# Second operands of an MoE input product: split straight out of PSUM or passed through DRAM as ready hi and lo pairs

## The chip, the cores and the metric

The kernel runs on one core of one Trainium2 chip. Its engines work side by side, each through its own queue in order: TensorE (PE, matrix products into PSUM), VectorE (DVE), ScalarE (ACT), GpSimd (POOL), and SyncE (SP), which issues the DMAs here. The metric is the device time of one execution in microseconds.

## The reference

An attention without learned projections over 8 batches of 8 heads (S = 512 tokens x, Ns = 32 state rows, D = 64) is read both ways, its heads are put side by side, and the rows go through a two-layer network with a squared ReLU:

```python
scores = scale * np.matmul(x, state.transpose(0, 1, 3, 2))
a = softmax(scores);  xread = np.matmul(a, state)         # 512 rows a batch
scores2 = scale * np.matmul(state, x.transpose(0, 1, 3, 2))
a2 = softmax(scores2);  sread = np.matmul(a2, x)          # 32 rows a batch
x = concat(xread, sread) as (8 * 544) rows of 512
h = np.maximum(x @ w_in, 0.0)                             # w_in 512 x 2048
return (h * h @ w_out).astype(np.float32)                 # w_out 2048 x 512
```

x and state come as float32, w_in and w_out as float64.

## The kernel before, in words

Every product is made of three TensorE matmuls (`mm3`): each fp32 operand is split into a hi part, which one fp32r holds, and a lo part, the rest; hi by hi, hi by lo and lo by hi are summed in PSUM. A split (`split`, lines 302 to 304) is a cast on ScalarE for hi and a subtraction on POOL or VectorE for lo.

The read of x by the states is folded into w_in: for a batch, `a @ (state @ w_in)` takes the place of `(a @ state) @ w_in`. The product of a batch's states with w_in is called **W2**, a matrix of 256 rows (8 heads of 32 state rows) by 2048 columns. There are nine blocks of tokens: block b, 0 to 7, is the x read of batch b (512 tokens, two operand tiles of 128 rows from W2), and block 8 the 256 rows of the state reads of all batches (four tiles of 128 rows of w_in itself). A block runs through 16 column chunks `fc` of 128: `hidden` makes the squared ReLU of a chunk with six matmuls of 512 columns (block 8: twelve of 256), splits it into g_hi (ScalarE, line 743) and g_lo (VectorE, line 744), and `accumulate` adds its product with w_out's rows into four PSUM banks (twelve matmuls of 512). Blocks 0 and 1 run chunks 0 to 7 first and park their sums in DRAM (`part_d`), then chunks 8 to 15.

w_in comes in 16 pieces p of 256 rows by 256 columns (two to a column block hb of 256). `load_raw` loads one, `decode_wi` turns its float64 words into fp32 with one ScalarE and four VectorE operations (lines 332 to 336) and stores it to DRAM (`win_d`). The 16 pieces of w_out are decoded the same way (`prep_wo`, tile names deco and wo).

W2 is made in one of two ways. **Direct** (`split_wi`, `direct_w2`): the piece is split, and the states of two batches stand in block-diagonal form, six matmuls of 256 columns for a p; ScalarE copies the result from PSUM (tile w2o), SyncE stores it in `w2a_d`. For batch 0 the copy is split on the spot; for others `load_w2` loads it back (tile w_f) and splits it. **Quad** (`quad_load`, `quad_prep`, `quad_w2`): the hi of 64 rows stands over the lo of the same 64 rows in one tile (tt), and four batches' states are multiplied at once, eight matmuls of 256 for a p; the results (qo) go to DRAM, are loaded and split. Batches 0 and 1 with 6 and 7 use the first way for p 0 to 7; for p 8 to 15 the quad (6, 7, 0, 1). Batches 2 to 5 are a quad throughout. `load_wi` loads pieces of w_in for block 8 in another row order and splits them.

The order of the work is written by hand: `PLAN` is a text that lists the steps in the order in which they are traced, and `step` checks their needs; the tile framework then sets the order on each engine by a cost model of its own. `SECOND` names the steps whose second choice of engine is taken (a split's subtraction on VectorE in place of POOL).

## Time and profile before

| | |
|---|---|
| median of 3 runs | 746.01 us (744.4 to 748.93) |
| profiled execution | 745.6 us, span 743.8 us |
| mean granted clock of TensorE | 0.970 |
| busy PE, DVE, ACT, POOL | 689.0, 450.0, 425.8, 252.6 us |
| moved by DMA | 94.10 MB |

A line of a profile names an engine, an operation, the tile that it writes and those that it reads, the shape, and how many; `ph` is a hidden chunk in PSUM, `acc` an accumulator, `w2ps` and `qps` the PSUM tiles of the two ways of W2, `k` the attention weights, `dec` a decoded piece of w_in, `xn` the tokens for the state read. L304 is line 304, a split's subtraction, which all splits share; so the tile names tell them apart. "idle before" is time in which that engine stood, with the work that ended it.

### The profile page before, as it was taken

Reading aid. Unit: us, or ns where it says so; the run is one execution under the profiler, and the core shown is the slowest. Engines: PE = TensorE matmul, PEld = TensorE weight load, DVE = VectorE, ACT = ScalarE, POOL = GpSimd, SP = SyncE. Lnnn points to the kernel's source line nnn. Section 1 sums busy time; section 2 is a strip of 40 time slices with the busy share of each in tenths; the row PEclk is TensorE's granted clock in tenths of the full one; section 3 lists DMA queues with packets and bytes.
Section 4 is the critical chain, followed back from the end, with each engine's and each line's share of the span. In section 5 each row is a group of like instructions: output and inputs, shape, how many; then the busy total and the mean of one; then the engine's idle time right before and its main releaser. Section 6 shows DMA issues by size and latency. Waiting matters only on the chain.

```text
span 743.8 us, 9790 instructions
## 1 busy us (share of the span) xinstructions
PE 689.0 (93%) x3240; PEld 568.6 (76%) x3240; DVE 450.0 (60%) x735; ACT 425.8 (57%) x824; POOL 252.6 (34%) x214
## 2 busy tenths in 40 slices
...
GB/s 267 210 197 183 189 188 254 212 139 231 147 210 222 114 240 115 149 123 148 66 100 83 145 92 65 57 113 80 35 57 143 29 42 57 128 58 71 15 1 85
DMA packets 85331, 94.10 MB, mean 127 GB/s; under 512 B 27681, under 2 KB 59425, under 8 KB 85281
## 3 DMA queue, kind: packets, MB, share of 16 engines
...
q8 instruction: 25, 0.41, 0.2%
...
## 4 chain that ended last, share of the span: by engine, by line
PE 63%; DVE 17%; DMA 7%; issue 5%; ACT 4%; SPq 2%; POOL 1%; DVEq 0%; ACTq 0%; POOLq 0%
PE acc L322 37%; PE ph L322 19%; PE pr L322 2%; DVE dec L335 2%; DVE deco L335 2%; DMA w_f<-w_d 2%; DVE g_lo L744 1%; DMA w_d<-qo 1%; PE st L322 1%; DVE deco L336 1%; DVE dec L333 1%; DVE dec L336 1%; PE w2ps L322 1%; DVE tt L676 1%; DMA wo_raw<-in_moe_w_out_dram 1%
## 5 line engine op out<-in xcount | busy, mean ns | idle before, releaser
L322 PE MATMUL acc<-wo,g_hi 128*128 128x512 f32 x1088 | 321.4, 398 | 16.7 <-ACT g_hi L743 15.5
L322 PEld LDWEIGHTS acc<-wo,g_hi 128*128 128x128 f32 x1088 | 205.4, 192 | 60.7 <-ACT g_hi L743 17.3
L322 PE MATMUL acc<-wo,g_lo 128*128 128x512 f32 x544 | 189.6, 392 | 0.0
L744 DVE TENSOR_TENSOR g_lo<-ph,g_hi 128x512 fp32r<-128x512 f32 (+1 forms) x144 | 94.3, 655 | 102.1 <-ACT g_hi L743 101.5
L322 PEld LDWEIGHTS acc<-wo,g_lo 128*128 128x128 f32 x544 | 102.0, 190 | 20.8 <-issue 0.5
L742 DVE SCALAR_TENSOR_TENSOR ph<-ph,r 128x512 f32<-128x512 f32 (+1 forms) x98 | 65.2, 666 | 79.9 <-ACT r L741 79.4
L743 ACT CAST g_hi<-ph 128x512 fp32r<-128x512 f32 (+1 forms) x144 | 80.8, 563 | 56.7 <-DVE ph L742 54.9
L322 PE MATMUL ph<-k_hi,w_hi 128*128 128x512 f32 x256 | 102.5, 402 | 10.6 <-DVE g_lo L744 8.3
L322 PE MATMUL ph<-k_lo,w_hi 128*128 128x512 f32 x256 | 101.2, 395 | 0.4 <-DVE k_lo L304 0.4
L322 PE MATMUL ph<-k_hi,w_lo 128*128 128x512 f32 x256 | 100.5, 393 | 0.3 <-POOL w_lo L304 0.3
L304 POOL TENSOR_TENSOR w_lo<-w_f,w_hi 128x512 fp32r<-128x512 f32 x39 | 51.9, 1331 | 137.9 <-ACT w_hi L303 134.3
L741 ACT ACTIVATE r<-ph 128x512 f32<-128x512 f32 (+1 forms) x98 | 56.3, 575 | 50.3 <-PE ph L322 49.9
L303 ACT CAST w_hi<-w_f 128x512 fp32r<-128x512 f32 x60 | 37.2, 621 | 67.2 <-PE ph L322 45.5
L322 PEld LDWEIGHTS ph<-k_hi,w_hi 128*128 128x128 f32 x256 | 48.5, 190 | 23.4 <-DVE g_lo L744 8.7
L322 PEld LDWEIGHTS ph<-k_hi,w_lo 128*128 128x128 f32 x256 | 48.6, 190 | 11.1 <-POOL w_lo L304 0.7
L322 PEld LDWEIGHTS ph<-k_lo,w_hi 128*128 128x128 f32 x256 | 48.8, 190 | 9.7 <-DVE k_lo L304 0.8
L676 POOL TENSOR_TENSOR tt<-decq,tt 64x512 fp32r<-64x512 f32 x16 | 21.3, 1331 | 46.7 <-ACT tt L673 27.9
L737 ACT ACTIVATE ph<-ph 128x512 f32<-128x512 f32 (+1 forms) x46 | 25.4, 553 | 16.2 <-PE ph L322 16.0
L304 POOL TENSOR_TENSOR xn_lo<-xn,xn_hi 128x1024 fp32r<-128x1024 f32 x10 | 24.4, 2439 | 26.0 <-ACT xn_hi L303 19.9
L304 POOL TENSOR_TENSOR x_lo<-xT,x_hi 128x512 fp32r<-128x512 f32 x11 | 14.8, 1342 | 51.6 <-DVE sp L424 32.5
L304 POOL TENSOR_TENSOR s<-decs,s 128x512 fp32r<-128x512 f32 x12 | 16.3, 1367 | 38.5 <-ACT s L303 38.4
L686 PE MATMUL qps<-tt,s_hi 128*128 128x256 f32 x96 | 25.6, 291 | 1.6 <-DVE qo L312 1.4
...
## 6 DMA issues: line engine op xcount, KB each, us to landing
w_d<-qo SPq DMA_DIRECT2D x96, 128.0 KB, 2.2
w_f<-w_d SPq DMA_DIRECT2D x48, 256.0 KB, 2.8
wo_raw<-in_moe_w_out_dram SPq DMA_DIRECT2D x16, 512.0 KB, 5.0
wi_raw<-in_moe_w_in_dram SPq DMA_DIRECT2D x16, 512.0 KB, 4.2
out_dram<-o SPq DMA_DIRECT2D x32, 256.0 KB, 3.9
xp<-in_x_dram SPq DMA_DIRECT2D x48, 128.0 KB, 2.6
decq<-win_d SPq DMA_DIRECT2D x24, 256.0 KB, 2.6
xn<-in_x_dram SPq DMA_DIRECT2D x12, 512.0 KB, 3.6
```

What stands on the lines that cost most here:

```text
L303: nc.scalar.copy(hi, src)
L304: pick(key, nc.gpsimd, nc.vector).tensor_sub(lo, src, hi.bitcast(F32))
L322: m = nc.tensor.matmul(ps, l, r, start=first and i == 0, stop=last and i == len(seq) - 1)
L335: nc.vector.scalar_tensor_tensor(v, high, 0xC0000000, v, ALU.bitwise_and, ALU.bitwise_or)
L336: nc.vector.scalar_tensor_tensor(v, low, 29, v, ALU.logical_shift_right, ALU.bitwise_or)
L676: eng.tensor_sub(t[v, :, i], wf[u], t[u, :, i].bitcast(F32))
L686: nc.tensor.matmul(ps[:, h2], s4_hi[:, h], t[:, c, h2], start=True, stop=False)
L737: nc.scalar.activation(ph, ph, AF.Relu)
L741: nc.scalar.activation(r, ph, AF.Relu)
L742: nc.vector.scalar_tensor_tensor(ph, ph, 0.0, r, ALU.max, ALU.mult)
L743: nc.scalar.copy(ghi, ph)
L744: nc.vector.tensor_sub(glo, ph, ghi.bitcast(F32))
```

## The change

w_in passes through DRAM as hi and lo: `split_wi` splits all 16 pieces once (POOL makes the lo of all but the first), and its tile, twice the bytes, is what is stored to `win_d`. What is loaded from there needs no conversion: `quad_load` puts the quad's operand together with four loads of 64 partitions, `load_wi` fills hi and lo with eight loads a tile pair, and `quad_prep` is gone.

For batches 0 and 1, p 0 to 7, `direct_w2` multiplies with the whole block-diagonal states, twelve matmuls of 256 columns for a p, and splits the result out of PSUM: hi by a ScalarE copy, lo by a VectorE subtraction, 128x256 for each batch. Batch 1's tiles lie in the buffers of w_out's last four pieces, whose loads therefore stand behind block 1's hidden chunks 1, 3, 5 and 7. For p 8 to 15 of batches 0 and 1, and for all p of batches 6 and 7, `paired_w2` takes six matmuls, splits out of PSUM (128x512) and stores hi and lo; `load_w2` then loads pairs without a split. Batches 2 to 5 remain a quad, with their split after the load. By count TensorE has 80 matmuls more (of 256 columns), VectorE 733 instructions for 737, ScalarE 719 for 810, POOL 152 for 219, and SyncE 608 DMAs for 484. After 250 us of the old trace the added steps are the 16 `qload.2`/`qw2.2` (eight before, with `qprep.2`).

```diff
-    hidden.0.1 scores.1.0 load_wo.5 load_w2.1.0 transposed_scores.1.0 load_raw.4 decode_wi.4 prep.1.1
-        accumulate.0.0 load_raw.5 load_wo.6 prep_wo.3 decode_wi.5
+    hidden.0.1 scores.1.0 load_wo.5 transposed_scores.1.0 load_raw.4 decode_wi.4 prep.1.1 accumulate.0.0
+        load_raw.5 load_wo.6 prep_wo.3 decode_wi.5
...
-    w_in_lo: 0.0 1.0 1.1 1.2 1.3 1.4
+    w_in_lo: 0
...
-    win_d = tc.dram_tile([NHB, NC // 2, P, 2, HB], F32, name="win_d")
-    w2_d = [
-        tc.dram_tile([4, 4, Ns, G, HB], F32, name=f"w2_d{q}_{hb}") for q in range(2) for hb in range(NHB)
-    ]
+    win_d = tc.dram_tile([NHB, NC // 2, P, 2, 2, HB], F32, name="win_d")
+    w2_d = [tc.dram_tile([4, 4, Ns, G, HB], F32, name=f"w2_d{hb}") for hb in range(NHB)]
     w2a_d = [
-        [tc.dram_tile([G, P, 2, HB], F32, name=f"w2a_d{i}_{hb}") for hb in range(DH)] for i in range(2)
+        [tc.dram_tile([G, P, 2, 2, HB], F32, name=f"w2a_d{i}_{hb}") for hb in range(NHB)] for i in range(2)
     ]
...
+    def prep_direct():
+        for b in range(2):
+            v = slice(NC * b, NC * b + NC)
+            split(s4_hi[:, v], s4_lo[:, v], bd_f[b], f"s4.d.{b}")
...
-    def prep_direct():
-        for b in range(2):
-            split(halves_of(s4_hi, b), halves_of(s4_lo, b), halves_of(bd_f[b], 0), f"s4.d.{b}")
-    def later_states(st, b0):
+    def paired_states(st, b0):
         stT = transposed_direct(st, b0)
         for t in (s4_hi, s4_lo):
             nc.gpsimd.memset(t[:, :NC].bitcast(F32), 0.0)
...
                 n = slice(32 * h2, 32 * h2 + 32)
                 hi, lo = (halves_of(t, b)[q, :, :, n] for t in (s4_hi, s4_lo))
                 src = stT[q, NC * b : NC * b + NC].rearrange("p (a c) n -> p a c n", c=2)
-                split(hi, lo, src, f"s4.e.{b}.{h2}")
+                split(hi, lo, src, f"s4.{b0}.{b}.{h2}")
     tt = {}
...
         tt[p] = raw
     def decode_wi(p):
-        wf = decode(tt.pop(p), [2, HB], p)
-        nc.sync.dma_start(win_d[p // 2, p % 2], wf)
-        tt[p] = wf
-    def split_wi(p, i=0):
-        w = p2.tile([P, 2, 2, HB], F32R, tag="tt", name=f"wi{i}_{p}", bufs=3)
-        split(w[:, 0], w[:, 1], tt.pop(p), f"w_in_lo.{i}.{p}")
+        tt[p] = decode(tt.pop(p), [2, HB], p)
+    def split_wi(p):
+        w = p2.tile([P, 2, 2, HB], F32R, tag="tt", name=f"wi{p}", bufs=3)
+        split(w[:, :, 0], w[:, :, 1], tt.pop(p), f"w_in_lo.{p}")
+        nc.sync.dma_start(win_d[p // 2, p % 2], w.bitcast(F32))
         tt[p] = w
-    def w2_tiles(b, hb):
-        return [
-            p2.tile([P, G, HB], F32R, tag=t, name=f"{t}{b}_{hb}", bufs=3) for t in ("w2_hi", "w2_lo")
-        ]
-    def direct_w2(p, i=0):
+    def w2_tile(b, hb):
+        return p2.tile([P, G, 2, HB], F32R, tag="w2", name=f"w2_{b}_{hb}", bufs=3)
+    def hi_lo(w):
+        return w[:, :, 0], w[:, :, 1]
+    def direct_w2(p):
         hb, g = divmod(p, 2)
         w = tt.pop(p)
-        whi, wlo = w[:, 0], w[:, 1]
+        ps = ps_b.tile([P, 2, HB], F32, tag="psb", name=f"w2ps{p}")
+        for b in range(2):
+            pairs = [2 * g + c for c in range(2)]
+            mm3(
+                ps[:, b],
+                [((s4_hi[:, NC * b + k], s4_lo[:, NC * b + k]), (w[:, c, 0], w[:, c, 1])) for c, k in enumerate(pairs)],
+            )
+        if g == 0:
+            first[0, hb] = w2_tile(0, hb)
+            first[1, hb] = cp.tile([P, G, 2, HB], F32R, tag=f"wo{NFC - DH + hb}", name=f"w2_1_{hb}")
+        for b in range(2):
+            t = first[b, hb]
+            nc.scalar.copy(t[:, g, 0], ps[:, b])
+            nc.vector.tensor_sub(t[:, g, 1], ps[:, b], t[:, g, 0].bitcast(F32))
+            weights[b, hb] = hi_lo(t)
+    def paired_w2(i, p):
+        hb, g = divmod(p, 2)
+        w = tt.pop(p)
         ps = ps_b.tile([P, 2, HB], F32, tag="psb", name=f"w2ps{i}_{p}")
         for c in range(2):
             k = 2 * g + c
-            mm3(ps[:, c], [((s4_hi[:, k], s4_lo[:, k]), (whi[:, c], wlo[:, c]))])
-        o = p2.tile([P, 2, HB], F32, tag="o", name=f"w2o{i}_{p}", bufs=4)
-        evac(f"w2_out.{i}.{p}", o, ps)
-        nc.sync.dma_start(w2a_d[i][hb][g], o)
-        if i == 0 and 2 * hb < HF:
-            if g == 0:
-                weights[0, hb] = w2_tiles(0, hb)
-            hi, lo = weights[0, hb]
-            for c in range(2):
-                q = slice(64 * c, 64 * c + 64)
-                split(hi[q, g], lo[q, g], o[q, c], f"w2_first.{p}.{c}")
+            mm3(ps[:, c], [((s4_hi[:, k], s4_lo[:, k]), (w[:, c, 0], w[:, c, 1]))])
+        hi, lo = [p2.tile([P, 2, HB], F32R, tag="o", name=f"w2{t}{i}_{p}", bufs=4) for t in ("h", "l")]
+        nc.scalar.copy(hi, ps)
+        nc.vector.tensor_sub(lo, ps, hi.bitcast(F32))
+        for j, o in enumerate((hi, lo)):
+            nc.sync.dma_start(w2a_d[i][hb][g, :, :, j], o.bitcast(F32))
...
-            wf = p2.tile([P, 2, HB], F32, tag="dec", name=f"decs{hb}_{i}", bufs=3)
             for h in range(4):
-                rows = win_d[hb, i][64 * (h % 2) : 64 * (h % 2) + 64, h // 2]
-                nc.sync.dma_start(wf[32 * h : 32 * h + 32], rows.rearrange("(e d) f -> d e f", e=E))
-            split(hi[:, 2 * i : 2 * i + 2], lo[:, 2 * i : 2 * i + 2], wf, f"s_lo.{hb}.{i}")
+                rows = win_d[hb, i][64 * (h % 2) : 64 * (h % 2) + 64, h // 2].rearrange("(e d) j f -> d e j f", e=E)
+                for j, t in enumerate((hi, lo)):
+                    nc.sync.dma_start(t[32 * h : 32 * h + 32, 2 * i : 2 * i + 2].bitcast(F32), rows[:, :, j])
...
-    quads = [(6, 7, 0, 1), (2, 3, 4, 5)]
+    quads = [None, (2, 3, 4, 5)]
     def quad_load(q, p):
-        wf = p2.tile([P, 2, HB], F32, tag="dec", name=f"decq{q}_{p}", bufs=3)
-        nc.sync.dma_start(wf, win_d[p // 2, p % 2])
-        tt[p] = wf
-    def quad_prep(q, p):
-        wf = tt.pop(p)
         t = p2.tile([P, 2, 2, HB], F32R, tag="tt", name=f"tt{q}_{p}", bufs=3)
-        h0, h1 = slice(0, 64), slice(64, 128)
-        nc.scalar.copy(t[h0, :, 0], wf[h0])
-        nc.scalar.copy(t[h1, :, 1], wf[h1])
-        for i, (u, v) in enumerate(((h0, h1), (h1, h0))):
-            eng = pick(f"quad_lo.{q}.{p}.{i}", nc.gpsimd, nc.vector)
-            eng.tensor_sub(t[v, :, i], wf[u], t[u, :, i].bitcast(F32))
+        tf, src = t.bitcast(F32), win_d[p // 2, p % 2]
+        if q == 1:
+            for j in range(2):
+                for h2 in range(2):
+                    v = slice(64 * h2, 64 * h2 + 64)
+                    nc.sync.dma_start(tf[64 * j : 64 * j + 64, :, h2], src[v, :, j])
+        else:
+            nc.sync.dma_start(tf, src)
         tt[p] = t
...
     def load_w2(b, hb):
-        raw = p2.tile([P, G, HB], F32, tag="dec", name=f"w2_f{b}_{hb}", bufs=3)
-        if b not in quads[1] and hb < DH:
+        w = w2_tile(b, hb)
+        weights[b, hb] = hi_lo(w)
+        if b not in quads[1]:
             for c in range(2):
                 q = slice(64 * ((b + c) % 2), 64 * ((b + c) % 2) + 64)
-                nc.sync.dma_start(
-                    raw[64 * c : 64 * c + 64], w2a_d[b > 1][hb][:, q, c].rearrange("g p f -> p g f")
-                )
+                nc.sync.dma_start(w[64 * c : 64 * c + 64].bitcast(F32), w2a_d[b > 1][hb][:, q, c].rearrange("g p j f -> p g j f"))
         else:
-            q = 0 if b in quads[0] else 1
-            bi = quads[q].index(b)
-            nc.sync.dma_start(raw, w2_d[q * NHB + hb][bi].rearrange("h n g f -> (h n) g f"))
-        hi, lo = w2_tiles(b, hb)
-        split(hi, lo, raw, f"w2_lo.{b}.{hb}")
-        weights[b, hb] = (hi, lo)
+            raw = p2.tile([P, G, HB], F32, tag="dec", name=f"w2_f{b}_{hb}", bufs=3)
+            nc.sync.dma_start(raw, w2_d[hb][quads[1].index(b)].rearrange("h n g f -> (h n) g f"))
+            split(*weights[b, hb], raw, f"w2_lo.{b}.{hb}")
...
+        late = [key("hidden", 1, 2 * (fc - NFC + DH) + 1)] if fc >= NFC - DH else []
+        step(key("load_wo", fc), load_wo, fc, after=late)
...
-                if blk or hb >= DH:
+                if blk > 1 or hb >= DH:
```

Three places show how instructions move. The first is VectorE's queue early in the program, from the decoding of w_in's second piece on (dec1 is that piece, dec2 the third; sp0_0, m10_0 and m20_0 belong to the softmax of batch 0). Before:

```order
L333 TENSOR_SCALAR dec1_242<-dec1_242 128x512
L334 TENSOR_SCALAR dec1_242<-dec1_242 128x512
L335 SCALAR_TENSOR_TENSOR dec1_242<-wi_raw1_130,dec1_242 128x512
L336 SCALAR_TENSOR_TENSOR dec1_242<-wi_raw1_130,dec1_242 128x512
L344 STREAM_TRANSPOSE stT2_1097<-st2_1095 128x128
L424 STREAM_TRANSPOSE sp0_0_158<-st0_0_155 128x512
L431 TENSOR_REDUCE m20_0_209<-st0_0_155 128x1
L454 TENSOR_REDUCE m10_0_160<-sp0_0_158 128x16
```

And now, where w2_0_0 and w2_1_0 are the first W2 tiles of batches 0 and 1:

```order
L329 TENSOR_SCALAR dec1_245<-dec1_245 128x512
L330 TENSOR_SCALAR dec1_245<-dec1_245 128x512
L331 SCALAR_TENSOR_TENSOR dec1_245<-wi_raw1_130,dec1_245 128x512
L332 SCALAR_TENSOR_TENSOR dec1_245<-wi_raw1_130,dec1_245 128x512
L615 TENSOR_TENSOR w2_0_0_232<-w2ps0_219,w2_0_0_232 128x256
L533 STREAM_TRANSPOSE stdT0_857<-std0_852 128x256
L329 TENSOR_SCALAR dec2_257<-dec2_257 128x512
L420 STREAM_TRANSPOSE sp0_0_158<-st0_0_155 128x512
L427 TENSOR_REDUCE m20_0_209<-st0_0_155 128x1
L615 TENSOR_TENSOR w2_1_0_233<-w2ps0_219,w2_1_0_233 128x256
```

The two subtractions of the first p stand ahead of most of the softmax of batch 0, behind the decoding of the second p.

The second place is VectorE at block 0's first two g_lo, which release its first accumulations (deco1, deco2 and deco3 are pieces of w_out, s11_0 and r21_0 belong to batch 1's softmax). Before:

```order
L446 RECIPROCAL r21_0_748<-r21_0_748 128x1
L744 TENSOR_TENSOR g_lo0_0_383<-ph0_0_375,g_hi0_0_382 128x512
L335 SCALAR_TENSOR_TENSOR deco3_516<-wo_raw3_351,deco3_516 128x512
L458 TENSOR_REDUCE s11_0_587<-sp1_0_472 128x16
L336 SCALAR_TENSOR_TENSOR deco3_516<-wo_raw3_351,deco3_516 128x512
L304 TENSOR_TENSOR w2_lo1_0_469<-w2_f1_0_465,w2_hi1_0_468 128x512
L459 TENSOR_SCALAR s11_0_587<-s11_0_587 128x16
L744 TENSOR_TENSOR g_lo0_1_455<-ph0_1_447,g_hi0_1_454 128x512
```

And now:

```order
L331 SCALAR_TENSOR_TENSOR deco1_396<-wo_raw1_110,deco1_396 128x512
L750 TENSOR_TENSOR g_lo0_0_391<-ph0_0_383,g_hi0_0_390 128x512
L750 TENSOR_TENSOR g_lo0_1_467<-ph0_1_459,g_hi0_1_466 128x512
L332 SCALAR_TENSOR_TENSOR deco1_396<-wo_raw1_110,deco1_396 128x512
L329 TENSOR_SCALAR deco2_450<-deco2_450 128x512
L330 TENSOR_SCALAR deco2_450<-deco2_450 128x512
L331 SCALAR_TENSOR_TENSOR deco2_450<-wo_raw2_251,deco2_450 128x512
L329 TENSOR_SCALAR dec4_481<-dec4_481 128x512
```

The first g_lo has moved from the 78th place on VectorE to the 67th, ahead of the decoding of w_out's pieces 2 and 3; the second stands right behind it, without the split of batch 1's W2 between them.

The third place is SyncE's queue at the load of w_out's thirteenth piece (wo_raw12; a name after "waits" is the engine or the DMA ring whose count it waits for). Before:

```order
L715 DMA wo_raw11_873<-in_moe_w_out_dram 128x1024 [waits DMAHW0_49]
L715 DMA wo_raw12_880<-in_moe_w_out_dram 128x1024 [waits DMAHW1_49]
L609 DMA w2a_d0_3_94<-w2o0_7_722 128x512 [waits DMAHW2_49,Activation_49]
L715 DMA wo_raw9_764<-in_moe_w_out_dram 128x1024 [waits DMAHW3_49]
L577 DMA wi_raw9_882<-in_moe_w_in_dram 128x2x512 [waits DMAHW4_49]
```

And now:

```order
L575 DMA wi_raw13_1179<-in_moe_w_in_dram 128x2x512 [waits DMAHW2_49,DVE_49]
L721 DMA wo_raw12_963<-in_moe_w_out_dram 128x1024 [waits DMAHW3_49,PE_49]
L784 DMA part_d0_99<-po0_1_1036 128x512 [waits DMAHW4_49,DVE_49]
L784 DMA part_d0_99<-po0_0_1033 128x512 [waits DMAHW5_49,Activation_49]
L587 DMA win_d_74<-wi11_1130 128x1024 [waits DMAHW6_49,Pool_49]
```

The load now waits for TensorE and stands behind the load of w_in's piece 13, where it stood ahead of piece 9's; the stores of block 0's parked sums come right behind it.

More of the change, by code (lines that the diff above doesn't have):

```diff
@@ L95 @@
     hidden.3.1 qload.2.1 accumulate.2.15
-    hidden.3.2 start.4 load_w2.3.3 qprep.2.1 accumulate.3.0
+    hidden.3.2 start.4 load_w2.3.3 accumulate.3.0
     hidden.3.3 prep.4.0 load.4.1 accumulate.3.1
@@ L103 @@
     hidden.3.9 transposed_scores.4.1 exp_s.4.1 qload.2.3 accumulate.3.7
-    hidden.3.10 softmax.4.1 load_w2.3.7 qprep.2.3 accumulate.3.8
+    hidden.3.10 softmax.4.1 load_w2.3.7 accumulate.3.8
     hidden.3.11 load_n.4.0 accumulate.3.9
@@ L107 @@
     hidden.3.13 qload.2.4 accumulate.3.11 sread.4.0
-    hidden.3.14 load_n.4.1 qprep.2.4 load_w2.4.1 accumulate.3.12
+    hidden.3.14 load_n.4.1 load_w2.4.1 accumulate.3.12
     hidden.3.15 transposes.4.1 accumulate.3.13
@@ L111 @@
     hidden.4.1 qload.2.5 accumulate.3.15
-    hidden.4.2 start.5 qprep.2.5 load_w2.4.3 accumulate.4.0
+    hidden.4.2 start.5 load_w2.4.3 accumulate.4.0
     hidden.4.3 prep.5.0 load.5.1 accumulate.4.1
@@ L119 @@
     hidden.4.9 exp_s.5.1 qload.2.7 accumulate.4.7
-    hidden.4.10 softmax.5.1 qprep.2.7 load_w2.4.7 accumulate.4.8
+    hidden.4.10 softmax.5.1 load_w2.4.7 accumulate.4.8
     hidden.4.11 load_n.5.0 accumulate.4.9
     hidden.4.12 transposes.5.0 qw2.2.7 load_w2.5.0 accumulate.4.10
-    hidden.4.13 accumulate.4.11 sread.5.0
+    hidden.4.13 qload.2.8 accumulate.4.11 sread.5.0
     hidden.4.14 load_n.5.1 load_w2.5.1 accumulate.4.12
-    hidden.4.15 transposes.5.1 accumulate.4.13
-    hidden.5.0 load_w2.5.2 accumulate.4.14 sread.5.1
+    hidden.4.15 qw2.2.8 transposes.5.1 accumulate.4.13
@@ L127 @@
+    hidden.5.0 qload.2.9 load_w2.5.2 accumulate.4.14 sread.5.1
     hidden.5.1 accumulate.4.15
-    hidden.5.2 start.6 load_w2.5.3 accumulate.5.0
-    hidden.5.3 prep.6.0 load.6.1 accumulate.5.1
+    hidden.5.2 qw2.2.9 start.6 load_w2.5.3 accumulate.5.0
+    hidden.5.3 qload.2.10 prep.6.0 load.6.1 accumulate.5.1
     hidden.5.4 load_w2.5.4 accumulate.5.2
-    hidden.5.5 scores.6.0 accumulate.5.3 transposed_scores.6.0
-    hidden.5.6 exp_s.6.0 prep.6.1 load_w2.5.5 accumulate.5.4
+    hidden.5.5 qw2.2.10 scores.6.0 accumulate.5.3 transposed_scores.6.0
```

127 lines of the change are left out of this document (63 added, 64 removed).

## The prediction

> **What bounds the kernel now.** I read the busy time by stretches first, then the chain of waits, the instruction lists where they pointed, and the groups by shape. The stretches of 25 us (start and end, length, busy time of PE, PE's weight loads, DVE, ACT and POOL with instruction counts, granted clock, DMA share, GB/s):
>
> ```profile
> core 0: us, PE busy (x) PEld busy (x) DVE busy (x) ACT busy (x) POOL busy (x), PEclk, DMA share, GB/s
> 0.00:25.00 25.00, 13.43 (x49) 8.15 (x49) 16.51 (x35) 17.29 (x41) 11.17 (x21) 1.00 0.96 284
> 25.00:50.00 25.00, 16.70 (x61) 12.11 (x62) 24.45 (x46) 18.38 (x39) 9.13 (x10) 0.77 0.69 210
> 50.00:75.00 25.00, 21.95 (x90) 16.67 (x89) 24.86 (x37) 16.62 (x35) 19.83 (x19) 0.89 0.47 148
> 75.00:100.00 25.00, 12.15 (x44) 9.09 (x42) 23.98 (x30) 13.34 (x24) 16.32 (x13) 0.66 0.56 177
> ...
> 150.00:175.00 25.00, 21.20 (x103) 16.76 (x102) 21.29 (x32) 14.18 (x26) 8.67 (x6) 1.00 0.53 146
> ...
> 200.00:225.00 25.00, 21.55 (x108) 17.64 (x106) 17.94 (x27) 14.44 (x25) 4.98 (x5) 1.00 0.65 211
> 225.00:250.00 25.00, 23.73 (x108) 20.20 (x109) 9.57 (x15) 12.87 (x24) 11.94 (x8) 0.86 0.54 168
> ...
> 400.00:425.00 25.00, 25.00 (x123) 21.11 (x122) 10.27 (x17) 14.19 (x28) 4.03 (x4) 1.00 0.43 140
> ```
>
> Two kernels stand here in one. At 400 us TensorE is busy without a gap at full clock: a matmul added there costs its own time, and work taken from another engine there is worth nothing. From 25 to 100 us it is VectorE that is full (73.3 of 75 us), and TensorE idles: 35.8 of its first 100 us, with a lower clock on top. From 200 to 250 TensorE stands 4.7 us, and neither VectorE nor POOL is full: those are waits. The same view as one stretch:
>
> ```profile
> 0.00:175.00 175.00, 129.10 (x534) 97.66 (x535) 157.89 (x243) 116.19 (x231) 89.89 (x84) 0.89 0.65 204
> ```
>
> VectorE works 157.9 of the first 175 us. The longest stop of TensorE, with VectorE and POOL at the same time:
>
> ```profile
> 88.10 3.78 PE L322 MATMUL acc<-wo,g_hi 128*128 128x512 f32 x8 [11.61 <-ACT g_hi L743]
> ...
> 85.75 0.68 DVE L336 SCALAR_TENSOR_TENSOR deco<-wo_raw,deco 128x512 uint32<-128x512 uint32 x1
> 86.36 0.41 DVE L333 TENSOR_SCALAR deco<-deco 128x512 f32<-128x512 f32 x1
> 86.69 0.41 DVE L334 TENSOR_SCALAR dec<-dec 128x512 uint32<-128x512 uint32 x1
> 87.03 1.75 DVE L334 TENSOR_SCALAR deco<-deco 128x512 uint32<-128x512 uint32 x1
> ...
> 86.81 3.45 POOL L304 TENSOR_TENSOR s_lo<-sqT,s_hi 128x512 fp32r<-128x512 f32 x2 [1.86 <-issue]
> ```
>
> TensorE waited 11.6 us for block 0's first activation while VectorE decoded weights. The same shape took 0.41 us at 86.69, and 1.75 at 87.03, when POOL had begun a subtraction. So POOL's work lengthens VectorE's. How much in all, by the four lines of the decoding, each 32 times in the first 175 us (DVE's busy time of lines 333, 334, 335, 336):
>
> ```profile
> 0.00:175.00 175.00, 22.34 (x32) 0.89 0.65 204
> 0.00:175.00 175.00, 21.70 (x32) 0.89 0.65 204
> 0.00:175.00 175.00, 33.98 (x32) 0.89 0.65 204
> 0.00:175.00 175.00, 27.66 (x32) 0.89 0.65 204
> ```
>
> They sum to 105.7 us; at 0.41, 0.41, 0.68 and 0.68 apiece they would be 69.8. The 35.9 us between, over POOL's 89.9 us of work, are 0.40 us of VectorE per us of POOL.
>
> **The change part by part.** Prices come from these groups (count | busy, mean ns):
>
> ```profile
> L304 POOL TENSOR_TENSOR w_lo<-w_f,w_hi 128x512 fp32r<-128x512 f32 x39 | 51.9, 1331 | 137.9 <-ACT w_hi L303 134.3 <-PE acc L322 3.1 <-DMA wo_raw<-in_moe_w_out_dram 0.2
> L676 POOL TENSOR_TENSOR tt<-dec,tt 64x512 fp32r<-64x512 f32 x14 | 19.2, 1373 | 20.4 <-ACT tt L672 15.9 <-ACT tt L673 4.1
> L304 POOL TENSOR_TENSOR w_lo<-w2o,w_hi 64x256 fp32r<-64x256 f32 x16 | 13.7, 859 | 5.6 <-ACT w_hi L303 4.8
> L304 POOL TENSOR_TENSOR wi<-dec,wi 128x512 fp32r<-128x512 f32 x7 | 9.8, 1399 | 17.1 <-ACT wi L303 16.9
> L744 DVE TENSOR_TENSOR g_lo<-ph,g_hi 128x512 fp32r<-128x512 f32 x128 | 87.5, 684 | 87.2 <-ACT g_hi L743 86.6
> L744 DVE TENSOR_TENSOR g_lo<-ph,g_hi 128x256 fp32r<-128x256 f32 x16 | 6.8, 424 | 14.9 <-ACT g_hi L743 14.9
> L312 DVE COPY qo<-qps 128x512 f32<-128x512 f32 x27 | 18.3, 680 | 12.9 <-PE qps L687 10.4 <-DMA out_dram<-o 2.2
> ```
>
> *POOL in the first 175 us.* Gone: the 16 half splits of batch 0's W2 (13.7), the 14 subtractions on decoded halves (19.2), three of batch 1's and 0's splits after the load (3 x 1.33 = 4.0), and the two quad-state subtractions of 86.81 (3.45). New: eight more w_in splits, 8 x 1.40 = 11.2, and the small block-diagonal states with their memsets, put at 3.5 as for the two subtractions that they replace. Net -25.6 us. At 0.40 that gives VectorE 10.2 back.
>
> *VectorE's own instructions there.* New: 16 subtractions of 128x256 out of PSUM (as g_lo of that size, 16 x 0.424 = 6.8) and 8 of 128x512 (8 x 0.684 = 5.5). Gone: seven evacuations (7 x 0.68 = 4.8) five splits (two on decoded halves, three after loads) and a transpose of the quad's states, put at 0.9 apiece for their contention with POOL, 5.4. Net +2.1. Together with the relief, -8.1 us; were the relief nil, +2.1, and were every us of POOL worth one of VectorE's, -23.5.
>
> The Trainium skill, "SBUF — State Buffer", Who interferes with whom, says that VectorE and GpSimd share a port pair as an exclusive lock and the loser is blocked fully, and that a VectorE operation with at most one SBUF input outside the faster modes does not contend. The trace agrees in kind: the PSUM-fed g_lo averages 0.684 us, no more than the undisturbed 0.68 of 85.75, while the decoding runs to four times 0.41. By that rule the added PSUM subtractions keep 0.42 and 0.68, and what POOL gives up is worth up to its full time; the row says 0.40, and the full price is a rival below.
>
> *New waits on VectorE's queue.* Each of the 16 subtractions waits for ScalarE's copy, that for twelve matmuls, and those for POOL's low part of w_in; behind it on VectorE stand the softmax of batch 0, the decoding and g_lo. TensorE's own wait for that low part stands in its list:
>
> ```profile
> 25.64 0.38 PE L322 MATMUL w2ps<-wi,s_hi 128*128 128x256 f32 x1 [2.03 <-POOL wi L304]
> ```
>
> Before, only ScalarE took the result. The two subtractions of a p come as a pair, so eight waits at most, 0 to 2.0 us each, 0 to 16 in all. By the order most stand several instructions behind their p's decoding, so I take 3.
>
> *TensorE.* 80 matmuls of 256 columns more: +48 for W2 of batches 0 and 1, -16 for the quad that went, +48 for batches 6 and 7. The chain of waits prices them, where TensorE runs dense (start, us, what, matmuls in a row):
>
> ```profile
> 217.71 5.59 DMA xn<-in_x_dram
> 224.53 2.34 POOL xn_lo L304
> ...
> 617.31 4.53 PE acc L322 x20
> ...
> 659.71 1.43 PE ph L322 x12
> ...
> 666.61 1.43 PE ph L322 x12
> ...
> 673.51 1.43 PE ph L322 x12
> ```
>
> 1.43/12 = 0.119 us for 256 columns, 4.53/20 = 0.2265 for 512. So +9.5 us of work. By the order of instructions, up to block 0's twelfth hidden part (where before TensorE still follows VectorE) TensorE has done 96 w2ps more, 60 qps fewer, and 11 matmuls of 512 more: 36 x 0.119 + 11 x 0.2265 = 6.8 us, which lie in its idle time (35.8 us in the first 100). The other 2.7 us come after it, on the path. If the idle time were not there, 9.5.
>
> *The waits of 200 to 250 us.* TensorE stands 4.7 us for the load of xn (5.59), POOL's split of it (2.34) and an evacuation. These engines lose the conversions of the operands (two casts and two subtractions for each p), and more W2 work of TensorE lies ahead of them: I take half of 4.7 with a little for the clock of 0.86, -2.5; bounds 0 and -8 (4.7 and 14% of 25).
>
> *ScalarE and what goes at no price.* It loses 91 instructions and was nowhere full (at most 18 of 25 us in the rows above); after 250 us POOL's and VectorE's savings are hidden behind TensorE. If TensorE's cover there broke, the loads would be why, as follows.
>
> *Transfers.* The issues (KB each, us to landing, and SyncE's time for eight):
>
> ```profile
> w_f<-w_d SPq DMA_DIRECT2D x48, 256.0 KB, 2.8
> wo_raw<-in_moe_w_out_dram SPq DMA_DIRECT2D x16, 512.0 KB, 5.0
> ...
> w_f<-w2a_d SPq DMA_DIRECT2D x24, 128.0 KB, 2.7
> ...
> 652.70 4.59 SPq L628 DMA_DIRECT2D decs<-win_d  x8
> ```
>
> SyncE issues 124 DMAs more, at 4.59/8 = 0.57 us. Four loads in place of one for batches 2 to 5 cost 4 x 0.57 = 2.3 us of SyncE against 0.57, for one p in some 5 to 14 us: hidden. w_in for block 8 takes 16 issues a column block, 9.2 us, in a period of 13.8 (the chain's ph at 659.71 and 673.51): hidden, with 4.6 to spare. The last four w_out loads now wait for hidden parts of block 1 on TensorE; SyncE's whole queue stands behind each, and a load lands in 5.0 us; their use is a pair of hidden parts and their accumulations later, 7 us or more. I put 0, with +8 as the bound (two of the four late by half their landing, and their followers with them).
>
> The Trainium skill, "DMA: Bandwidth & Descriptors", Rules for kernel authors, speaks against these loads: two transfers to separate halves of the partitions serialize, and one of 128 partitions should be used. The trace agrees so far that 128 KB take 2.7 us to land where 256 KB take 2.8. It lengthens a load that is hidden, and so adds nothing to the sum.
>
> Sum against the profiled execution, 745.6 us (span 743.8; the median of the runs, 746.0, is 0.4 above): VectorE's stretch -8.1 + 3 = -5.1, TensorE +2.7, the later waits -2.5, transfers 0: -4.9, so 741 us.
>
> **The rivals.** *The full port price (faster).* If VectorE gains a us for each us that POOL gives up, the stretch falls by 25.6 instead of 10.2: 741 - 15 = 726. For it: the 87.03 row, four times its length under POOL. Against: 0.40 over the stretch, since half of VectorE's work is of other kinds.
>
> *The 11.6 us stop goes (faster).* In the new order block 0's first two g_lo stand eleven rows earlier on VectorE. If what comes after is paced by these accumulations rather than by VectorE's total, eleven rows of 0.7 are 8 us: 733. Against: VectorE is full to 175 us, so what is passed over has still to be done.
>
> *The subtractions block VectorE (slower).* If each of the eight pairs holds VectorE for the 2.0 us that TensorE waits for POOL, it is +16 instead of +3: 754. It decides where the copy ends after VectorE has reached the subtraction, from about 15 of those 16 us on. For it: VectorE is the bound there and nothing can pass. Against: from hidden 0.0 on the queue has decoding ahead of them.
>
> *No relief, only work (same).* If the low parts of w_in, now POOL's alone, take from VectorE as much as the rest gives back (+2.1 +3), and the 2.7 and none of the waits: 753; with half of the relief 748. I take 749.
>
> *Issue-bound loads (slower).* If the 16 quarter loads take over 13.8 us a column block, 1 to 2 us late for each of eight: 749 to 757. Against: 9.2 us.
>
> **How the numbers follow.** A change of 1% is what a measurement here can tell: faster means below 738.5, slower above 753.5. The forecast has 0.42, of which 0.12 below 738.5; the full port price 0.12; the stop 0.14; no relief 0.14; blocked subtractions 0.14, 0.10 of it above 753.5; the loads 0.04, all slower. Faster 0.12 + 0.12 + 0.14 = 0.38, slower 0.14, same 0.48. Faster and same hold most of it: the likeliest case's own range is 735 to 748. The range for 8 in 10 leaves out the lower part of the full port price and the upper of the last rivals: 728 to 755.
>
> **What would show it.** VectorE's four decoding lines at less than 105.7 us in the first 175, and POOL near 64: the relief. TensorE's busy time up by about 9, with a first 100 us that holds some 6 more. The wait ahead of the new subtractions on VectorE, summed, near 3: the queue; near 16, the slower rival. Gaps in TensorE after 250 us that end on a DMA would show the loads wrong, and a stretch from 200 to 250 with 4.7 us idle again the waits. I am wrong if the first accumulation of block 0 begins no earlier than 88 us.

## The result and the profile after

The changed kernel takes 727.06 us (median of 4 runs, 725.51 to 729.87) where the kernel before takes 747.43 beside it: a ratio of 0.9737, 95% interval 0.969 to 0.9783. Run twice more with the experiments it took 730.07 (0.979, 0.9762 to 0.9817) and 731.18 us (0.9797, 0.9764 to 0.983). So it is 2.0 to 2.6% faster; 741 was forecast, and the range began at 728. The profiled execution's span went from 743.8 to 725.4 us, 18.4 less.

The stretches of 25 us of the changed kernel, columns as before:

```profile
0.00:25.00 25.00, 14.75 (x61) 10.09 (x61) 15.59 (x33) 14.69 (x35) 7.19 (x17) 1.00 0.94 267
25.00:50.00 25.00, 18.52 (x84) 13.92 (x84) 23.39 (x49) 16.05 (x33) 5.64 (x4) 0.93 0.74 220
50.00:75.00 25.00, 18.93 (x85) 13.87 (x84) 25.00 (x46) 16.52 (x36) 16.11 (x15) 0.93 0.55 180
75.00:100.00 25.00, 22.46 (x106) 18.06 (x105) 24.90 (x41) 18.31 (x40) 12.75 (x13) 0.93 0.42 132
100.00:125.00 25.00, 21.29 (x95) 17.37 (x94) 24.97 (x41) 16.49 (x30) 9.96 (x7) 0.93 0.93 318
125.00:150.00 25.00, 24.59 (x120) 20.57 (x119) 23.40 (x41) 16.55 (x33) 7.85 (x6) 1.00 1.00 328
150.00:175.00 25.00, 24.76 (x119) 20.70 (x118) 21.36 (x42) 15.22 (x30) 8.95 (x9) 1.00 0.91 252
...
200.00:225.00 25.00, 25.00 (x133) 21.44 (x132) 10.27 (x17) 11.58 (x22) 5.47 (x4) 1.00 0.80 240
225.00:250.00 25.00, 25.00 (x130) 21.39 (x129) 11.91 (x20) 10.13 (x20) 3.89 (x3) 1.00 0.63 201
250.00:275.00 25.00, 22.91 (x111) 18.47 (x110) 15.87 (x30) 10.74 (x20) 5.56 (x6) 1.00 0.76 227
275.00:300.00 25.00, 23.96 (x115) 19.70 (x114) 14.48 (x26) 18.07 (x38) 13.33 (x14) 1.00 0.55 177
```

TensorE is dense from 125 us on but for 250 to 300, where it was for good from 250 before. VectorE is as full as it was up to 150 us (and does more instructions in the time). From 200 to 250 us the 4.7 us of idle time and the clock of 0.86 are gone. From 250 to 300, where it had stood 0.0, TensorE now stands 3.1 us: a loss that was not there. In the first 100 us TensorE's busy time rose from 64.2 to 74.7 us; over the whole span it did not rise by the 9 us that the prediction named as a sign, it went from 689.0 to 688.8. Busy time counts a matmul that takes longer as more, so it does not show the added work.

The first 175 us as one stretch, and VectorE's four decoding lines in it (now 329 to 332):

```profile
0.00:175.00 175.00, 145.31 (x660) 114.58 (x661) 158.59 (x286) 113.82 (x232) 68.46 (x70) 0.96 0.78 242
...
0.00:175.00 175.00, 20.23 (x32) 0.96 0.78 242
0.00:175.00 175.00, 19.28 (x32) 0.96 0.78 242
0.00:175.00 175.00, 24.88 (x32) 0.96 0.78 242
0.00:175.00 175.00, 27.05 (x32) 0.96 0.78 242
```

VectorE is busy as long as before (157.9, now 158.6), with 286 instructions for 243. The decoding takes 91.4 us in place of 105.7.

A comparison by the clock hides how far each kernel has come. So I took the same point of work in both, the end of the 8th, 16th, 24th and 32nd g_lo, and counted up to it VectorE's busy time, POOL's busy time and TensorE's **lost time**: start to start of neighbouring matmuls, less 0.444 ns for each column (0.227 us for 512, as in the prediction's dense row), summed. It holds both standing and matmuls that took longer than that price. All from the two traces, in us:

| up to | time | VectorE busy | POOL busy | TensorE lost |
|---|---|---|---|---|
| 8th g_lo | 108.5 -> 101.9 | 95.8 -> 90.8 | 61.1 -> 42.3 | 55.0 -> 40.0 |
| 16th | 156.5 -> 141.4 | 143.1 -> 130.1 | 83.0 -> 56.9 | 66.2 -> 47.6 |
| 24th | 203.8 -> 180.7 | 184.3 -> 162.8 | 109.4 -> 68.5 | 71.5 -> 48.4 |
| 32nd | 251.9 -> 223.2 | 209.9 -> 180.6 | 124.5 -> 75.9 | 81.1 -> 49.0 |
| end | 743.8 -> 725.4 | 450.0 -> 416.6 | 252.6 -> 160.8 | 87.6 -> 59.8 |

The row of the 24th g_lo in the view of the stretches, before and after:

```profile
0.00:203.80 203.80, 157.90 (x673) 121.87 (x674) 184.31 (x285) 138.45 (x273) 109.45 (x100) 0.91 0.64 202
0.00:180.70 180.70, 151.01 (x689) 119.41 (x690) 162.76 (x292) 116.82 (x237) 68.46 (x70) 0.96 0.79 244
```

Of the 23.1 us by which this point comes earlier, VectorE's busy time makes up 21.5; the time that VectorE stood went only from 19.5 to 17.9.

TensorE's dense work (all its columns at 0.444 ns) grew from 645.1 to 654.2 us (+9.1), its lost time fell by 27.8: together -18.7, the change of the span within 0.3. By the pages' busy time, some 18.5 of the 27.8 is standing and 9.3 is matmuls that took longer, at a mean granted clock of 0.970 before and 0.991 now. To read off the table: 23.1 of lost time went by the 24th g_lo, 9.0 between the 24th and the 32nd, and 4.3 came back behind it.

The long stop of TensorE is gone; these are the longest that it now has between 30 and 110 us:

```profile
39.75 2.04 PE L318 MATMUL acc<-wo,g_hi 128*128 128x512 f32 x4 [3.71 <-ACT wo L299]
...
108.34 0.79 PE L318 MATMUL ph<-k_hi,w 128*128 128x512 f32 x1 [3.71 <-DVE g_lo L750]
```

The added operations have the durations of the rows from which they were priced (POOL's splits of w_in, VectorE's subtractions out of PSUM), and the wait ahead of the latter in the first 185 us is a single one:

```profile
L300 POOL TENSOR_TENSOR wi<-dec,wi 128x512 fp32r<-128x512 f32 x15 | 20.8, 1389 | 35.1 <-ACT wi L299 30.4 <-issue 4.7
L628 DVE TENSOR_TENSOR w2l<-w2ps,w2h 128x512 fp32r<-128x512 f32 x24 | 16.4, 683 | 11.9 <-ACT w2h L627 6.7 <-DMA out_dram<-o 5.1
L615 DVE TENSOR_TENSOR w<-w2ps,w 128x256 fp32r<-128x256 f32 x16 | 6.5, 412 | 1.4 <-ACT w L614 1.4
```

### The profile page after: what moved, and what is told of

Same layout as the page of the kernel before. It is cut to its first block, busy times and chain, and to the rows that moved or that the text cites. A ratio compares the mean times of both kernels' runs of the same rounds, so it can differ in the third digit from the quotient of the medians.

```text
span 725.4 us, 9875 instructions
## 1 busy us (share of the span) xinstructions
PE 688.8 (95%) x3320; PEld 572.4 (79%) x3320; DVE 416.6 (57%) x731; ACT 372.8 (51%) x733; POOL 160.8 (22%) x147
## 4 chain that ended last, share of the span: by engine, by line
PE 71%; DVE 14%; DMA 5%; issue 4%; SPq 3%; ACT 2%; POOL 1%; DVEq 0%; ACTq 0%; POOLq 0%
PE acc L318 41%; PE ph L318 21%; PE pr L318 2%; PE w2ps L318 2%; PE st L318 2%; DMA w_f<-w_d 1%; DMA xp<-in_x_dram 1%; DVE deco L331 1%; DVE dec L332 1%; DVE deco L330 1%; DVE g_lo L750 1%; DVE dec L331 1%; DVE deco L329 1%; DMA wo_raw<-in_moe_w_out_dram 1%; DVE deco L332 1%
## 5 line engine op out<-in xcount | busy, mean ns | idle before, releaser
L318 PE MATMUL ph<-k_hi,w 128*128 128x512 f32 x512 | 181.4, 396 | 6.7 <-DVE g_lo L750 5.6
L750 DVE TENSOR_TENSOR g_lo<-ph,g_hi 128x512 fp32r<-128x512 f32 (+1 forms) x144 | 94.5, 657 | 90.8 <-ACT g_hi L749 89.7
L748 DVE SCALAR_TENSOR_TENSOR ph<-ph,r 128x512 f32<-128x512 f32 (+1 forms) x98 | 65.4, 667 | 105.9 <-ACT r L747 105.7
L318 PEld LDWEIGHTS ph<-k_hi,w 128*128 128x128 f32 x512 | 96.3, 189 | 28.5 <-DVE g_lo L750 6.7
L318 PE MATMUL ph<-k_lo,w 128*128 128x512 f32 x256 | 100.5, 393 | 0.0
L318 PEld LDWEIGHTS ph<-k_lo,w 128*128 128x128 f32 x256 | 48.4, 189 | 9.8 <-DVE k_lo L300 0.4
L743 ACT ACTIVATE ph<-ph 128x512 f32<-128x512 f32 (+1 forms) x46 | 25.3, 553 | 45.2 <-PE ph L318 45.2
L300 POOL TENSOR_TENSOR w<-w_f,w 128x512 fp32r<-128x512 f32 x20 | 25.9, 1293 | 100.1 <-ACT w L299 100.1
L299 ACT CAST w<-w_f 128x512 fp32r<-128x512 f32 x32 | 19.7, 614 | 17.8 <-DMA w_f<-w_d 14.0
L300 POOL TENSOR_TENSOR wi<-dec,wi 128x512 fp32r<-128x512 f32 x15 | 20.8, 1389 | 35.1 <-ACT wi L299 30.4
L318 PE MATMUL w2ps<-wi,s_hi 128*128 128x256 f32 x96 | 21.7, 314 | 7.0 <-ACT wi L299 2.2
L744 ACT ACTIVATE ph<-ph 128x512 f32<-128x512 f32 (+1 forms) x46 | 25.4, 556 | 0.9
L318 PE MATMUL ph<-sr_hi,s 128*128 128x256 f32 x128 | 25.5, 282 | 0.0
```

The lines of the kernel that those rows point to most:

```text
L299: nc.scalar.copy(hi, src)
L300: pick(key, nc.gpsimd, nc.vector).tensor_sub(lo, src, hi.bitcast(F32))
L318: m = nc.tensor.matmul(ps, l, r, start=first and i == 0, stop=last and i == len(seq) - 1)
L743: nc.scalar.activation(ph, ph, AF.Relu)
L744: nc.scalar.activation(ph, ph, AF.Square)
L748: nc.vector.scalar_tensor_tensor(ph, ph, 0.0, r, ALU.max, ALU.mult)
```

## The experiments

The changed kernel was timed three times, at 727.06, 730.07 and 731.18 us, and a run is compared with the one beside it where there is one. Parts of an edit that are not shown are marked by dots.

**Theory** after the result: POOL's work stretches VectorE's (makes its instructions take longer) by a fixed share, VectorE holds back TensorE early on, and the change took much more of POOL's work out of that stretch than I had counted. **Rivals**: the full port price (a us of VectorE for each us of POOL), which had named 726; no price at all, the gain coming from order and fewer trips.

### POOL's work added, by reading and by writing alone

```diff
...
         nc.sync.dma_start(win_d[p // 2, p % 2], w.bitcast(F32))
+        lo = w[:, :, 1].bitcast(F32)
+        if p < 12:                       # idle: a tile that nobody reads
+            nc.gpsimd.tensor_sub(idle[0], lo, lo)
+            for _ in range(2):           # second kernel: range(5) and memset(idle[0], 0.0)
+                nc.gpsimd.tensor_sub(idle[0], lo, lo)
```

> The changed kernel (727 us) with 36 more subtractions of 128x512 on POOL, three behind each of the first twelve w_in splits, into a tile that nobody reads: about 36 x 1.35 = 49 us of POOL in the first 150 us. Theory (POOL's reading subtractions stretch VectorE, the bound there, by 0.40 to 0.48 us per us): +20 to +24, so 747 to 751. Rival, full port price (1 us per us): 775. Rival, POOL costs VectorE nothing and the gain came from fewer instructions and another order: 727 to 731.

> As the run with 36 subtractions, but only the first of each three is a subtraction, and five memsets of 0.53 us (which write and read nothing) take the time of the other two: 12 x 1.35 = 16 us of subtractions and 60 x 0.53 = 32 us of memsets. Theory (only POOL operations that read SBUF stretch VectorE): +7, so 734. Rival, any POOL work stretches it: 747 to 751, as with the subtractions. Rival, POOL costs VectorE nothing: 727 to 731.

The subtractions gave 761.12 us (1.0193 of before, 1.016 to 1.0225), the memsets 749.69 (1.0055, 1.003 to 1.008): 30 to 34 and 19 to 23 us above the changed kernel. The memsets write the tile and read nothing. The larger of the two added groups of POOL in the first and in the second kernel (twelve more subtractions, 14.7 and 14.0 us, stand beside each), and for each VectorE's first decoding line on w_out:

```profile
L596 POOL TENSOR_TENSOR idle<-wi 128x512 f32<-128x512 f32 x24 | 28.9, 1203 | 1.1
L329 DVE TENSOR_SCALAR deco<-deco 128x512 f32<-128x512 f32 x16 | 14.6, 914 | 0.1
```

```profile
L596 POOL MEMSET idle<- 128x512 f32 x60 | 34.8, 580 | 2.5
L329 DVE TENSOR_SCALAR deco<-deco 128x512 f32<-128x512 f32 x16 | 16.3, 1018 | 0.2 <-ACT deco L328 0.2
```

In the changed kernel the same line averages 643 ns:

```profile
L329 DVE TENSOR_SCALAR deco<-deco 128x512 f32<-128x512 f32 x16 | 10.3, 643 | 0.1
```

Up to the 24th g_lo POOL had 45 us more of reading work in the first kernel, and VectorE was busy 186.3 us where the changed kernel needs 162.8 to 164.2: 0.5 us per us. That is the upper end of the theory's price. This point came 24 to 27 us later, nearly all of it VectorE's busy time; the kernel's time grew by more, 30 to 34 us, as TensorE's lost time did (94.3 for 59.8 to 64.0). The other 5 to 7 us are lost behind the 24th g_lo. POOL's own queue is one candidate, which the expectation had left out: its last split of w_in began at 169.7 us in place of 141.6. That it is the cause is not shown. That only reading operations stretch VectorE is refuted: the memsets, which read nothing, did it too. With the price of 0.5 for the 14 us of subtractions beside them, the 34.8 us of memsets come to about 0.3 us per us (VectorE was busy 181.4 us up to the 24th g_lo). "No price" is out.

The Trainium skill, "SBUF — State Buffer", Who interferes with whom, makes a VectorE operation in the faster modes contend with any GpSimd operation, and one with two SBUF inputs only with a GpSimd operation that reads SBUF. The line that the memsets stretched most, 643 to 1018 ns, has a single input, which agrees with the first half of this. The third decoding line on w_out, with two inputs, rose too, from 820 to 1020 ns; subtractions ran beside the memsets, so the second half is not tested here.

### The low parts of w_in on VectorE

```diff
-    w_in_lo: 0
+    w_in_lo: 0 1 2 3 4 5 6 7 8 9 10 11 12 13 14 15
```

> The changed kernel with the lo part of all w_in pieces subtracted on VectorE: POOL loses 15 x 1.39 = 20.8 us, VectorE gets 15 x 0.68 = 10.2 us of its own. Theory (0.40 to 0.48 us per us of POOL): -8 to -10 and +10, so 727 to 729, no change. Rival, full port price: 716. Rival, POOL costs nothing: 737.

731.81 us (0.9807, 0.9778 to 0.9836), 1 to 5 us above the three times of the changed kernel, with an interval of the ratio that overlaps each of theirs: no gain and no clear loss, near what the theory had, and 16 us from the full port price. VectorE's busy time to the 24th g_lo was 161.6, as without it; the 15 subtractions that it took over were paid by its other work being less stretched.

### The kernel before with less of POOL's reading work

```diff
-            eng.tensor_sub(t[v, :, i], wf[u], t[u, :, i].bitcast(F32))
+            if q == 0 and eng is nc.gpsimd:
+                nc.gpsimd.memset(t[v, :, i].bitcast(F32), 0.0)
+            else:
+                eng.tensor_sub(t[v, :, i], wf[u], t[u, :, i].bitcast(F32))
```

(and so for the splits of batch 0's W2).

> The kernel before, with 30 of POOL's subtractions replaced by memsets to zero (the 16 half splits of batch 0's W2 and the 14 on the decoded halves for the quad; these lo parts are left out, so the values lose precision): 32.9 us of reading POOL work less, some 10 us of memsets in its place. Theory (0.40 to 0.48 per us of reading POOL work): 13 to 16 us less than before, 731 to 734. Rival, full port price: 714. Rival, POOL costs VectorE nothing: 746.

728.73 us (0.9774 of before, 0.9746 to 0.9802): 17 us from the kernel before alone, as much as the whole change brought in that group (730.07). Nothing of the changed plan, its trips through DRAM or its loads is in it. But the framework set the order on the engines anew (VectorE's first differs from the 77th instruction on), the memsets are shorter than the subtractions, and they do not wait for ScalarE's cast. What POOL did in the places of 32.9 us of subtractions:

```profile
L680 POOL MEMSET tt<- 64x512 f32 x14 | 7.9, 566 | 7.3 <-PE qps L693 6.6
L305 POOL MEMSET w_lo<- 64x256 f32 x16 | 5.4, 339 | 0.5
```

The row of the 24th g_lo here:

```profile
0.00:192.40 192.40, 156.52 (x684) 122.19 (x685) 172.38 (x288) 140.83 (x277) 93.59 (x101) 0.95 0.71 218
```

VectorE was busy 172.4 us up to the 24th g_lo instead of 184.3, 11.9 less, where POOL to that point had 29.1 us of reading work less and 13.4 of memsets more; by 0.5 and 0.3 that is 10.5. The point came 11.4 us earlier, and VectorE stood as long as before (20.0 us, before 19.5): what got shorter is VectorE's work, not its waits. TensorE's lost time was 68.6 for 87.6; 13.6 of the 19.0 are there by the 24th g_lo, the rest between it and the 32nd, in the stops of 200 to 250 us. So POOL's work of the first 200 us is enough for a gain of this size, and up to the 24th g_lo it comes through VectorE's busy time. The full port price, 714, is 15 us off.

### TensorE's added work, early and late

```diff
         for b in range(2):
+            if b:                        # batch 1 takes batch 0's result
+                break
             pairs = [2 * g + c for c in range(2)]
...
```

> The changed kernel with 48 of the 96 matmuls of the direct way left out (batch 1's first half of W2 is taken from batch 0's result, so those values are not the reference's): 48 x 0.119 = 5.7 us less on TensorE in the first 100 us. Theory (VectorE is the bound there, TensorE's added work lies in its idle time): 726 to 727, no change. Rival (TensorE's work counts there): 721.

```diff
-        for c in range(2):
+        for c in range(2 - i):           # batches 6 and 7: one half for both
             k = 2 * g + c
...
```

> The changed kernel with 48 of the 96 matmuls of the paired way for batches 6 and 7 left out (the second half of their W2 rows is taken from the first half's result, so those values are not the reference's): 48 x 0.119 = 5.7 us of TensorE after 300 us, where it is busy without a gap. Theory (it counts in full there): 5 to 6 us less than the changed kernel of this group. Rival (hidden, as in the first 100 us): no change.

Without 48 of the early matmuls: 732.29 us (0.9819, 0.9787 to 0.985), no gain, as if their 5.5 us lay in time that TensorE does not have work for. It is no clean test: the kernel is 1 to 5 us slower than the changed one, and VectorE was busy 167.4 us by the 24th g_lo, 3 to 5 more, for nearly the same POOL work. I have no cause for that beyond the new order, and it could hide a small gain. Without 48 of the late ones: 724.04 us (0.9697, 0.9664 to 0.9729), 7.1 less than the 731.18 beside it and 3.0 less than the fastest of the three: the late term counts, at about its price of 5.5.

### The direct way undone

The first half of batches 0 and 1 takes the paired way, with `load_w2` for its tiles in the plan, and w_out's last loads no longer wait:

```diff
-            step(key("direct_w2", p), direct_w2, p, ...
+            step(key("direct_w2", p), paired_w2, 0, p, ...
```

> One part undone: batches 0 and 1 take the paired way for the first half too (six matmuls for a p, split out of PSUM as 128x512, stored to DRAM as hi and lo and loaded back as pairs; w_out's last loads no longer wait). w_in's way and the rest stay as changed. Theory (the gain comes from POOL's work and the conversions that are gone, in which this does not differ; VectorE 8 x 0.68 for 16 x 0.41, 1 us less): 727 to 731, the trip through DRAM for batch 0's first tiles being partly hidden. Rival (the direct split out of PSUM, without the trip, is what made the gain): 738 or more.

737.08 us (0.9896, 0.9862 to 0.9929), 7.0 above the 730.07 beside it, nearer to the rival than to the theory. TensorE's waits in its first 115 us:

```profile
PE ph L318 <- DMA w<-w2a_d: 7.2, 2, 6.1
PE w2ps L318 <- DVE w2l L628: 5.1, 1, 5.1
```

The trip through DRAM stands ahead of a hidden chunk, 6.1 us at once. So the direct way is worth about 7 us beside the relief, although TensorE has 48 matmuls fewer without it. POOL had done 5 to 10 us more by the same points here, but VectorE's busy time up to the 24th g_lo was the same (163.8, and 163.9 in the changed kernel's run beside it), while VectorE stood 25.0 us in place of 18.1. The 7 us are waits, then, and the trip is the longest new one; how the rest hang on it was not followed.

### The operand by one load, and VectorE's work on ScalarE

For the loss of 250 to 300 us: w_in in DRAM with the order half, hi or lo, row, so that a quad's operand comes by one DMA; in turn the stores, and the later loads for batches 6 and 7, take two DMAs in place of one. Between 200 and 300 us SyncE issued 94 DMAs where it had issued 119.

```diff
...
-            for j in range(2):
-                for h2 in range(2):
-                    v = slice(64 * h2, 64 * h2 + 64)
-                    nc.sync.dma_start(tf[64 * j : 64 * j + 64, :, h2], src[v, :, j])
+            nc.sync.dma_start(tf, src.rearrange("h j d c f -> (j d) h c f"))
...
```

> The changed kernel with w_in's hi and lo stored in DRAM so that a quad's operand comes by one load of 128 partitions in place of four of 64 (48 issues less between 200 and 300 us; the stores and the later loads for batches 6 and 7 take two issues in place of one). Theory (the stops of 5.6 us between 250 and 300 us come from SyncE's queue, busy issuing loads and stores): 5 us less, so 722. Rival (they come from something else, the transfers themselves or VectorE): 727.

732.70 us (0.9829, 0.9803 to 0.9855), not less than 730.07. The loads, now of 512 KB and 5.0 us, and the four-part ones of the changed kernel:

```profile
tt<-win_d SPq DMA_DIRECT2D x16, 512.0 KB, 5.0
```

```profile
tt<-win_d SPq DMA_DIRECT2D x64, 128.0 KB, 3.3
```

TensorE still stood 3.6 us from 250 to 300 us (1.97 and 1.66 by its stretches): SyncE's issues for the operand are not the cause of most of it. In the changed kernel's second run VectorE, ahead of one of these stops of TensorE, waits for batch 3's tokens, whose last load SyncE issued behind one for W2 (VectorE, TensorE, SyncE):

```profile
292.79 0.71 DVE L372 STREAM_TRANSPOSE xT<-xp 128x512 f32<-128x512 f32 x1 [2.74 <-DMA xp<-in_x_dram]
...
294.77 2.42 PE L318 MATMUL acc<-wo,g_hi 128*128 128x512 f32 x6 [2.72 <-ACT g_hi L749]
...
288.20 0.34 SPq L712 DMA_DIRECT2D w_f<-w_d  x1
288.59 0.43 SPq L365 DMA_DIRECT2D xp<-in_x_dram  x1
```

For the first 180 us: squares of ten chunks and six evacuations from VectorE to ScalarE (the first kernel), and with it batch 2's xn_lo on VectorE, to free the buffer of those tokens earlier (the second).

```diff
-    eT: 0.1 1.0
-    part: 0.1 0.3 1.1 1.3
-    square: 0.0 0.1 0.2 0.3 0.4 0.5 0.6 0.7 0.13 1.4 1.9 ...
+    square: 0.0 0.1 0.2 0.3 0.4 0.5 0.6 0.7 0.8 0.9 0.10 0.13 1.0 1.1 1.2 1.3 1.4 1.5 1.6 1.7 1.9 ...
-    xn_lo: 5.1 6.1
+    xn_lo: 2.0 2.1 5.1 6.1               # second kernel only
```

> The changed kernel with VectorE work of the first 200 us given to ScalarE: the square of ten hidden chunks (block 0's 8 to 10, block 1's 0 to 3 and 5 to 7: 10 x 0.67 us), four evacuations of parked sums and two of transposes (6 x 0.68), about 10.8 us, most of it before 180 us. ScalarE gets about as much. Theory (VectorE's total bounds the kernel up to 180 us): 6 to 9 us less than the changed kernel of this group. Rival (ScalarE's queue or the order takes its place): no change.

> As the run with VectorE's work given to ScalarE, and the lo part of batch 2's state-read tokens on VectorE (1.23 us) in place of POOL (2.40), which frees the buffer for the load of batch 3's tokens earlier, on which VectorE waited 2.7 us at 293. Theory: 1 to 2 us less than without it. Rival (the load is late for SyncE's queue): no change.

> The changed kernel itself, as the base for the others of this group: 727 to 730.

734.81 us (0.9841, 0.9807 to 0.9876) and 735.19 (0.986, 0.9818 to 0.9902) beside 731.18: no gain, rather a loss of 4. VectorE was busy 156.1 us to the 24th g_lo in place of 164.2 and stood 25.3 instead of 18.7, and TensorE's lost time to there did not move (49.5, 50.4). My theory that VectorE bounds the changed kernel up to 180 us falls: TensorE loses next to nothing after about 125 us (24.59 and 24.76 of 25 us busy in the stretches from there), so what VectorE is spared later has nobody waiting. Nor did the earlier xn_lo help; what makes the stops of 250 to 300 us stays open.

The changed kernel again, as the base of the second group:

> The changed kernel itself, as the base for the others of this group: 727.

It took 730.07 us. No kernel of the study that computes the whole reference beats it.

## Why the prediction was right or wrong, point by point

The direction, the place and the mechanism were right, the size was not: -4.9 forecast, -18.4 in the spans. Three terms were too small: POOL's net, the price of its work, and the waits of 200 to 250 us.

**POOL's net of -25.6 us** is the first step that failed. By the same point of work it was -41.0 (109.4 to 68.5 at the 24th g_lo). I had counted to 175 us by the clock of the old trace, though TensorE lost time until 250 there. Six subtractions of the quad (2, 3, 4, 5) on loaded halves (8.4 us), three more splits behind loads than I had taken (4.8) and what else POOL did from 175 to 204 us belong to the stretch and were left out.

**The price of 0.40 us per us** was a little low too. In the traces of the study VectorE's stretch (busy time above that of its undisturbed instructions, an estimate by the shortest of each kind) over all of POOL's work was 0.37 to 0.50. Between two kernels the price was 0.5: the traces show a stretch of 50.6 and 29.5, 21 less for the 41 us, and the added subtractions gave the same. I had 10.2. The 15 us of POOL that I missed are about 6 of the difference, the price is the rest.

**VectorE's own instructions, +2.1**: 133.8 to 133.3 at the 24th g_lo, -0.5. (By the same undisturbed times.) A miss of 2.6 us, with the same fault of the end point. **New waits, +3**: 1.4 in one place; the decoding ahead of the subtractions covers the copies, as argued. The blocked queue did not come.

**TensorE**: +9.5 forecast, +9.1 by the 80 matmuls at 0.444 ns a column. That the late part is paid is shown by taking it away; that the early part is free agrees with its run, which is no clean test.

**The waits of 200 to 250 us, -2.5**: too small. All of the stops and the clock's fall went, 4.7 idle and the 0.86 of one stretch, which is the bound of 8 that I had written beside it; the lost time between the 24th and 32nd g_lo fell by 9.0. That is 6.5 more than I had, as large a miss as POOL's net. In the kernel before with memsets for its subtractions most of these stops went too, so they hang on POOL's work of the time before. By which path is not shown: before the change they ended on VectorE's copy of qo, ScalarE's cast of xn and POOL's split of xn.

**Transfers, 0**: w_out's last loads cost nothing visible, and w_in for block 8 nothing: from 330 us on TensorE's lost time is 4.5 in the changed kernel and 4.2 before. But 3 to 4 us of new stops came between 250 and 300. One of them stands behind the load of batch 3's tokens, the others behind other work, and making the operand's four loads one did not remove them; their cause stays open.

**The rivals.** The full port price gave 726 and the time was 727, but by the wrong price: it asked for 716 and 714 where 732 and 729 were measured. No relief and issue-bound loads did not come. The 11.6 us stop is gone, but the lead is 6.6 us at the 8th g_lo and grows to 15, 23 and 29 with each eight more, so it is not one stop's worth. And I had tied that stop to the wrong place. It was not block 0's first accumulation that waited until 88.10; that began at 47.33 (TensorE before):

```profile
47.33 3.78 PE L322 MATMUL acc<-wo,g_hi 128*128 128x512 f32 x8 [2.15 <-ACT g_hi L743]
```

The first g_lo, which the order showed eleven places earlier, ended at 48.9 us before and ends at 40.6 now; the stop at 88.10 stood ahead of the fifth. So my test "no earlier than 88 us" was set against a wrong reading, and that the first accumulation begins at 39.75 confirms nothing.

In the terms of lost time, I had -14.4 (6.8 absorbed, 5.1 and 2.5), and -27.8 came: 11 of the difference up to the 24th g_lo, 6.5 in the waits behind it, 4 given back later.
